# 384 rows of w_out loaded apart, by two queues, with other engines and another order of use

## The chip, the core and the metric

One Trainium2 chip, of which the program uses one core. The metric is the device time of the program in microseconds (us). A core has TensorE (PE in the profile, with its weight loads as PEld), VectorE (DVE), ScalarE (ACT), GpSimd (POOL) and SyncE (SP), and 16 DMA engines that all queues share. SP and ACT issue transfers through hardware queues (q1 and q10 in the profile), GpSimd through a software queue (q0). q8 and q14 carry instruction packets, which the program does not issue.

## The reference

A single token `x` (1 x 576, bfloat16) is normalised and goes through two branches, whose results are added to it.

```python
xn = layernorm(x)                                  # 576
# A: attention with a window of the cache
q  = xn @ wq                                       # 576 -> 32 heads x 128
k, v = k_cache[:, :, -4096:], v_cache[:, :, -4096:]  # 16 kv heads, each for 2 heads
a  = softmax(q k^T * 128**-0.5) v                  # 32 x 128
A  = a.reshape(4096) @ wo                          # -> 576
# B: gated MLP
z  = gelu(xn @ w_in)                               # 576 -> 4608
z1, z2 = z[:2304], layernorm(z[2304:])
B  = (z1 * (w_sp * z2 + b_sp)) @ w_out             # 2304 -> 576
out = x + A + B
```

Nearly all bytes are weights and cache that are read once: wq, the windows of k and v, w_in, wo and w_out, 51 MB together.

## The kernel before, in words

**Loads.** Everything large is loaded by SP, in one order written out by hand at the top of the kernel: wq in two loads, k0, k1, v0, k2, v1, k3, win, v2, v3, wo in two loads, and w_out in four (`load`, line 96). The four k and v blocks hold four kv heads each. Two pools of two buffers each hold these tiles (`small` and `large`); a load waits until the tile that had its buffer before has been read. So `wo` waits for the last z product, which reads `win`, and `wout` for the last transposition of k3. A transfer of 128 partitions is shared out over all 16 DMA engines, eight partitions each.

**w_out.** SP loads rows 384 to 2303 (before: 256 to 2303), with partition p holding FR consecutive rows side by side. In before that is FR = 16 rows a partition, cut after 8, 13 and 15. The first rows of w_out are loaded apart: in before GpSimd loads 160 of them to partitions 64 to 79 (line 393) and ScalarE 96 to partitions 0 to 11 (line 396), both to columns behind the other FR rows. These columns are zeroed first by GpSimd (line 391), since TensorE reads all 128 partitions of them. Two very small transfers of GpSimd (`skip`, line 388) write to columns that nothing reads; they stand ahead of its load and behind it.

**Stages.** For each block b, `turn(b)` transposes k on VectorE (line 214), `scores(b)` makes the scores and the softmax (lines 259 to 285), `weigh(b)` multiplies the weights with v (line 293) and copies the sum to SBUF on ScalarE (line 298), and `heads(b)` adds up the parts of each head (line 304) and scales it on VectorE (line 307). The calls stand in a fixed order, and each engine works through its own instructions in the order of the program:

turn 0, scores 0, turn 1, scores 1, values 0 (weigh and heads), turn 2, scores 2, values 1, turn 3, the zeroing and GpSimd's transfers, scores 3, ScalarE's transfer, `z_all`, weigh 2, `gate`, heads 2, the rows of w_out loaded apart, values 3, o_x and o_p (the attention's output as columns), the 32 rows of wo, the FR rows of w_out, the output.

**z and gate.** `z_all` multiplies the token with w_in in nine rounds r (line 323). Four column groups of TensorE (`tile_position`) take 512 columns each; the columns that belong to the 256 rows apart go to a second PSUM tile, 96 in group 0 and 160 in group 2. VectorE copies the results to SBUF (lines 332 and 334) into 32 x 32 blocks and transposes these (lines 338 and 339), so that z stands by partition as w_out does; row j of a 32 x 32 block comes out as partition j. `gate` computes the gelu, the second norm and the product `hv`, one column for each of the FC = 26 row sets.

**The sum.** `row_of` (line 406) adds one row set to the output: two matmuls of a column with 288 columns of weights each, in two column groups, into two PSUM tiles `fin`. The last row set of w_out closes the sum; VectorE and ScalarE copy the two halves (lines 430 and 431), and SP and ScalarE store them.

Of the kernel before, what the change touches and what calls it, by code (L numbers as in the profile page):

```python
# [8 lines left out]
FP32 = mybir.dt.float32  # L9
# [5 lines left out]
P = 128  # L15
D = 576
# [5 lines left out]
FH = 2304  # L22
# [7 lines left out]
EPS = 1e-5  # L30
SCALE = DH ** -0.5
GELU_C = 0.7978845608028654
FR = 16
FA, RA = 96, 8
FB, RB = 160, 10
FE = FA + FB
FC = FR + RB
FQ = 512
WR = HQ * DH // P
HW = D // 2  # L40
ZPAD = 24
# [6 lines left out]
def kernel(  # L48
# [14 lines left out]
    nc = tc.nc  # L63
# [4 lines left out]
    one = ctx.enter_context(tc.tile_pool(name="one", bufs=1))  # L68
# [19 lines left out]
    def unit(name, width):  # L88
        pool = small if width == SMALL else large
        return pool.tile([P, width], BF16, name=name, tag="u")  # L90
# [4 lines left out]
    def load(t, view, width, cuts):  # L95
        for a, e in zip(cuts, cuts[1:]):
            nc.sync.dma_start(t[:, (a - cuts[0]) * width:(e - cuts[0]) * width], view[:, a * width:e * width])
# [23 lines left out]
    wo_t = unit("wo", LARGE)  # L121
    load(wo_t, wo_v, D, (0, 20, WR))
    wout_t = unit("wout", SMALL)
    load(wout_t, B_w_out[FE:FH, :].rearrange("(p r) n -> p (r n)", r=FR), D, (0, 8, 13, 15, FR))


    ident = const.tile([P, P], BF16, name="ident")
# [1 line left out]
    xw = const.tile([P, NR, 32], BF16, name="xw")  # L129
# [46 lines left out]
    def rstd_of(stats_ps, n, name):  # L176
        mv = const.tile([P, 4], FP32, name=name)
        nc.vector.tensor_scalar_mul(mv[:, 0:2], stats_ps, 1.0 / n)
        nc.vector.tensor_mul(mv[:, 2:3], mv[:, 0:1], mv[:, 0:1])
        nc.vector.tensor_sub(mv[:, 2:3], mv[:, 1:2], mv[:, 2:3])  # L180
        nc.scalar.activation(mv[:, 2:3], mv[:, 2:3], ACT.Ln, bias=eps_t[:, 0:1])
        nc.scalar.activation(mv[:, 3:4], mv[:, 2:3], ACT.Exp, scale=-0.5)
        return mv
# [103 lines left out]
    def weigh(b):  # L287
        pv = ps_v.tile([P, 512], FP32, name=f"pv{b}", tag="pv")
        v4 = vn[b][:, 0:NU * DH].rearrange("p (k n u d) -> p k u n d", k=2, n=4, d=DH)
        for kk in range(2):  # L290
            for u in range(UK):
                g = u % 4
                nc.tensor.matmul(  # L293
                    pv[32 * g:32 * g + 32, :].rearrange("p (n d) -> p n d", n=4), lhsT=p_t[b][:, kk, u, :],
                    rhs=v4[:, kk, u, :, :], start=kk == 0 and u < 4, stop=kk == 1 and u >= UK - 4,
                    tile_position=(0, 32 * g))
        pvs = one.tile([P, 512], FP32, name=f"pvs{b}", tag="pvs")
        nc.scalar.copy(pvs[:], pv[:])  # L298
        return pvs

    def heads(b, pvs):
        op = ps_m.tile([P, 8], FP32, name=f"op{b}", tag="m")
        for u in range(4):
            nc.tensor.matmul(op[:], lhsT=pvs[:, DH * u:DH * (u + 1)], rhs=selu[:, 8 * u:8 * u + 8],  # L304
                             start=u == 0, stop=u == 3)
        with nc.allow_low_precision(reason="the attention's output is bfloat16 in the reference"):
            nc.vector.tensor_tensor(out=o_t[:, 8 * b:8 * b + 8], in0=op[:], in1=rms[b][:], op=ALU.mult)  # L307

    def values(b):
        heads(b, weigh(b))  # L310


    hv = const.tile([P, FC], BF16, name="hv")


    def z_all():
        zs = one.tile([P, FQ + 32 * RB], FP32, name="zs", tag="sm")
        nc.gpsimd.memset(zs[:, FQ:], 0.0)
        zx = zs[:, FQ:].rearrange("p (r i) -> p r i", i=32)
        zp = [ps_a.tile([P, FQ], FP32, name=f"z{i}", tag="a") for i in range(2)]  # L320

        def product(i, g, r, a, n, to):
            nc.tensor.matmul(zp[i][32 * g:32 * g + 32, to:to + n], lhsT=xw[:, r, :],  # L323
                             rhs=win_t[:, FH * r + a:FH * r + a + n],
                             start=r == 0, stop=r == NR - 1, tile_position=(0, 32 * g))

        for r in range(NR):
            for g in range(4):
                product(0, g, r, FE + FQ * g, FQ, 0)
            product(1, 0, r, 0, FA, 0)  # L330
            product(1, 2, r, FA, FB, FA)
        nc.vector.tensor_copy(zs[:, 0:FQ], zp[0][:])
        for q, n, a, rows, k in ((0, 12, 0, RA, 3), (64, 16, FA, RB, 4)):
            nc.vector.tensor_copy(
                zx[q:q + 32, 0:rows, 0:n].rearrange("p r (i x) -> p r i x", x=4),
                zp[1][q:q + 32, a:a + n * rows].rearrange("p (x i r) -> p r i x", x=4, i=k))
        zt = one.tile([P, FC, 32], FP32, name="zt", tag="zt")
        nc.vector.transpose(zt[:, 0:FR, :], zs[:, 0:FQ].rearrange("p (i r) -> p r i", r=FR))
        nc.vector.transpose(zt[:, FR:, :], zx)
        return zt[:, :, 0:2]  # L340

    def gate(z):
        def t3(name):
            return const.tile([P, FC, 2], FP32, name=name)

# [8 lines left out]
        nc.vector.reciprocal(e[:], e[:])  # L354
        G = const.tile([P, 2, FC], FP32, name="G")
        nc.vector.tensor_mul(G[:].rearrange("p h c -> p c h"), e[:], z)
        sz = const.tile([P, 2], FP32, name="sz")
        nc.vector.tensor_reduce(out=sz[:, 0:1], in_=G[:, 1, :], axis=AXX, op=ALU.add)
        jz = const.tile([P, FC], FP32, name="jz")
        nc.vector.tensor_tensor_reduce(out=jz[:], in0=G[:, 1, :], in1=G[:, 1, :], scale=1.0, scalar=0.0,  # L360
# [3 lines left out]
        mz = rstd_of(sp[:], FH, "mz")  # L364
        gz = const.tile([P, FC], FP32, name="gz")
        nc.vector.tensor_scalar(out=gz[:], in0=G[:, 1, :], scalar1=mz[:, 0:1], scalar2=mz[:, 3:4],
# [14 lines left out]

    def blocks(a, e, k):
        return B_w_out[a:e, :].rearrange("(x i r) n -> i x (r n)", x=4, i=k)

    def skip(k, a):
        nc.gpsimd.dma_start(wout_t[0:k, a:a + 32].rearrange("i (m c) -> i m c", m=2),
                            B_w_out[0:2 * k, 0:16].rearrange("(m i) n -> i m n", m=2))

    nc.gpsimd.memset(wout_t[:, D * FR:D * FC], 0.0)  # L391
    skip(8, D * FC)
    nc.gpsimd.dma_start(wout_t[64:80, D * FR:D * FC], blocks(FA, FE, 4))
    skip(4, D * FC + 32)
    scores(3)
    nc.scalar.dma_start(wout_t[0:12, D * FR:D * (FR + RA)], blocks(0, FA, 3))
    z = z_all()
    pvs2 = weigh(2)
    gate(z)
# [4 lines left out]
    def row_of(col, w, start=False, stop=False):  # L404
        for g in range(2):
            nc.tensor.matmul(fin[g][32 * g:32 * g + 1, :], lhsT=col, rhs=w[:, HW * g:HW * (g + 1)],  # L406
                             start=start, stop=stop, tile_position=(0, 32 * g))

    row_of(one_bf[:, 0:1], x_row, start=True)
    for r in range(FR, FC):  # L410
        row_of(hv[:, r:r + 1], wout_t[:, D * r:D * (r + 1)])
    values(3)


    o_x = const.tile([P, 32], BF16, name="o_x")
# [47 lines left out]
```

## Time and profile before

| | |
|---|---|
| median of 3 runs | 127.32 us (127.17 to 127.56) |
| the profiled execution | 127.1 us |
| its span, from the first to the last instruction | 125.3 us |
| mean granted TensorE clock | 0.845 |
| busy: PE, DVE, POOL, ACT | 62%, 52%, 9%, 8% of the span |
| bytes read | 50.96 MB, 407 GB/s over the span |

The profile shows one execution. Its busy slices cut the span into 40 equal parts and give each engine's busy share in tenths. The chain of waits is followed back from the last instruction: at each step to what released it. A line of the timeline is start, duration, engine, source line, operation and tile. The DMA rows are mean shares over 16 engines. The trace also keeps every DMA packet with its start, duration, bytes and queue, and the time of every semaphore increment that a transfer leaves.

### The profile page before, as it was taken

The numbers are of one execution on the slowest core, as the hardware profiler recorded it, in microseconds if no ns is written. First come the engines' busy times: TensorE is split into PE (matmuls) and PEld (weight loads), VectorE is DVE, ScalarE is ACT, GpSimd is POOL, SyncE is SP. The second block draws the span as 40 slices with busy tenths as digits, with TensorE's granted clock in tenths as the row PEclk, the third lists the DMA queues.
The fourth block names the chain that finished last, engine by engine and source line by source line (L and its number), as shares of the span: only waits on it lengthen the run. The fifth ranks groups of instructions, "written<-read, shape, count | busy, mean of one in ns | idle before, by whom it ended". The sixth has DMA issues, their size and how long they took to land.

```text
span 125.3 us, 1324 instructions
## 1 busy us (share of the span) xinstructions
PE 77.9 (62%) x528; PEld 39.3 (31%) x532; DVE 65.0 (52%) x131; ACT 10.2 (8%) x19; POOL 11.0 (9%) x15
## 2 busy tenths in 40 slices
PE   0233550099823999197499637499459434977971
PEld 0231220034311333044234224134148222543640
DVE  6336033499839994340899541999540952001001
ACT  3010000000030000301000031000030110010001
POOL 8400000000000000000000000000992000000000
PEclk9999999999996579855559999779995995586798
DMA  3999899997989989899998999999898999999960
GB/s 107 511 430 439 353 502 418 418 492 345 502 377 447 481 366 481 366 471 429 418 492 356 520 434 424 416 388 471 377 481 359 467 394 433 449 393 415 410 260 0
DMA packets 2624, 51.03 MB, mean 407 GB/s; under 512 B 411, under 2 KB 543, under 8 KB 799
## 3 DMA queue, kind: packets, MB, share of 16 engines
q1 hardware_dynamic: 2450, 50.66, 94.7%
q0 software_dynamic: 144, 0.19, 0.4%
q10 hardware_dynamic: 25, 0.11, 0.2%
q8 instruction: 4, 0.07, 0.2%
q14 instruction: 1, 0.01, 0.0%
HBM read 50.96 MB, written 0.00 MB: 407 GB/s over the span
## 4 chain that ended last, share of the span: by engine, by line
PE 43%; DMA 36%; DVE 10%; ACT 4%; issue 3%; SPq 1%; ACTq 0%
PE s L259 29%; DMA wout<-in_B_w_out_dram 18%; DMA k<-in_A_k_cache_dram 18%; PE pv L293 4%; DVE kt L214 4%; PE z L323 3%; ACT p L279 3%; PE op L304 2%; DVE sm L262 2%; PE tr L270 2%; PE fin L406 1%; PE su L283 1%; DVE pt L281 1%; DVE m L272 1%; ACT pvs L298 1%
## 5 line engine op out<-in xcount | busy, mean ns | idle before, releaser
L259 PE MATMUL s<-kt,zq 128*128 128x512 bf16 x124 | 36.8, 458 | 11.8 <-DVE kt L214 11.1
L214 DVE STREAM_TRANSPOSE kt<-k 128x1024 f32<-128x1024 f32 x32 | 36.4, 1206 | 3.9 <-DMA k<-in_A_k_cache_dram 3.9
L259 PEld LDWEIGHTS <-zq 128*128 128x128 bf16 x128 | 14.5, 113 | 33.0 <-issue 22.4
L391 POOL MEMSET wout<- 128x5760 bf16 x1 | 4.9, 4897 | 83.2 <-DVE kt L214 83.2
L293 PE MATMUL pv<-v,pt 128*32 128x512 bf16 x128 | 11.9, 498 | 0.0
L279 ACT ACTIVATE p<-sm,nm 128x1024 bf16<-128x1024 f32 x4 | 4.6, 1147 | 69.9 <-DVE nm L275 69.9
L307 DVE TENSOR_TENSOR o_t<-op,rm 128x8 bf16<-128x8 f32 x4 | 0.7, 165 | 16.6 <-PE op L304 16.6
L281 DVE STREAM_TRANSPOSE pt<-p 128x1024 bf16<-128x1024 bf16 x4 | 5.0, 1245 | 5.4 <-ACT p L279 5.4
L262 DVE CUSTOM_DVE_ANT_1 sm<-s,cm 128x512 f32<-128x512 f32 x8 | 5.4, 673 | 4.0 <-PE s L259 4.0
L223 PE MATMUL q_ps<-wq,xw 128*32 128x512 bf16 x36 | 4.2, 626 | 4.7 <-DMA wq<-in_A_wq_dram 2.4
L293 PEld LDWEIGHTS <-pt 128*32 128x32 bf16 x128 | 5.7, 119 | 3.8 <-issue 2.4
L304 PE MATMUL op<-selu,pvs 128*128 128x8 f32 x32 | 5.1, 287 | 2.5 <-ACT pvs L298 2.1
L283 PE MATMUL su<-sel,l 128*128 128x8 f32 x8 | 1.8, 292 | 7.7 <-ACT p L279 7.7
L406 PE MATMUL fin<-wout,hv 128*1 128x288 bf16 x52 | 5.1, 344 | 2.3 <-DMA wout<-in_B_w_out_dram 2.3
L304 PEld LDWEIGHTS op<-selu,pvs 128*128 128x128 f32 x32 | 4.8, 228 | 4.4 <-ACT pvs L298 4.0
L406 PE MATMUL fin<-wo,o_p 128*1 128x288 bf16 x64 | 5.7, 353 | 0.3 <-DVE o_p L420 0.3
L430 DVE CAST res<-fin 1x288 bf16<-1x288 f32 x1 | 0.4, 446 | 8.8 <-PE fin L406 8.8
L161 PE MATMUL x_ps<-one_bf,x_row 1*64 1x1 bf16 x9 | 1.2, 248 | 5.6 <-DMA x_row<-in_A_x_dram 5.6
L323 PE MATMUL z<-win,xw 128*32 128x512 bf16 (+2 forms) x54 | 4.4, 448 | 0.0
L270 PE MATMUL tr<-ident_f,m 128*128 128x128 f32 x8 | 1.9, 326 | 3.9 <-DVE m L268 3.9
L406 PEld LDWEIGHTS <-o_p 128*1 128x1 bf16 x64 | 3.3, 101 | 3.1 <-DVE o_p L420 1.0
L406 PEld LDWEIGHTS <-hv 128*1 128x1 bf16 x52 | 2.6, 95 | 4.5 <-issue 3.0
(94 smaller groups left out, 44.4 us busy)
## 6 DMA issues: line engine op xcount, KB each, us to landing
k<-in_A_k_cache_dram SPq DMA_DIRECT2D x4, 4096.0 KB, 21.5
v<-in_A_v_cache_dram SPq DMA_DIRECT2D x4, 4096.0 KB, 26.6
win<-in_B_w_in_dram SPq DMA_DIRECT2D x1, 5184.0 KB
wq<-in_A_wq_dram SPq DMA_DIRECT2D x1, 3584.0 KB, 12.8
wo<-in_A_wo_dram SPq DMA_DIRECT2D x1, 2880.0 KB
wo<-in_A_wo_dram SPq DMA_DIRECT2D x1, 1728.0 KB, 19.4
wout<-in_B_w_out_dram SPq DMA_DIRECT2D x1, 1152.0 KB
wq<-in_A_wq_dram SPq DMA_DIRECT2D x1, 1024.0 KB, 4.8
```

Of the source, the lines that this page charges most:

```text
L214: nc.vector.transpose(t[:].rearrange("p c n e -> p (c n e)").bitcast(FP32), kn[b][:, UK * DH * k:UK * DH * (k + 1)].bitcast(FP32).rearrang ...
L223: nc.tensor.matmul(q_ps[32 * g:32 * g + 32, :], lhsT=xw[:, r, :], rhs=wq_t[:, 2048 * r + 512 * g:2048 * r + 512 * (g + 1)], start=r == 0, ...
L259: nc.tensor.matmul(s_ps[:], lhsT=zq[:, b, ce, ZPAD - 8 * k4:ZPAD - 8 * k4 + P], rhs=kt[b, 4 * kk + k4][:, c, :, e], start=k4 == 0 and ce = ...
L262: nc.vector.tensor_tensor_reduce(out=sm[:, kk, :].rearrange("p (n s) -> p n s", s=HB), in0=s_ps[:].rearrange("p (n s) -> p n s", s=HB), in ...
L270: nc.tensor.matmul(tr[:], lhsT=m1[:].to_broadcast([P, P]), rhs=ident_f[:], start=True, stop=True)
L279: nc.scalar.activation(p[:], sm[:].rearrange("p k n -> p (k n)"), ACT.Exp, bias=nm[:], accum_out=l[:])
L281: nc.vector.transpose(p_t[b][:].rearrange("p k u m -> p (k u m)"), p[:])
L293: nc.tensor.matmul(pv[32 * g:32 * g + 32, :].rearrange("p (n d) -> p n d", n=4), lhsT=p_t[b][:, kk, u, :], rhs=v4[:, kk, u, :, :], start=k ...
L304: nc.tensor.matmul(op[:], lhsT=pvs[:, DH * u:DH * (u + 1)], rhs=selu[:, 8 * u:8 * u + 8], start=u == 0, stop=u == 3)
L323: nc.tensor.matmul(zp[i][32 * g:32 * g + 32, to:to + n], lhsT=xw[:, r, :], rhs=win_t[:, FH * r + a:FH * r + a + n], start=r == 0, stop=r = ...
L391: nc.gpsimd.memset(wout_t[:, D * FR:D * FC], 0.0)
L406: nc.tensor.matmul(fin[g][32 * g:32 * g + 1, :], lhsT=col, rhs=w[:, HW * g:HW * (g + 1)], start=start, stop=stop, tile_position=(0, 32 * g))
```

## The change

- Instead of 256 rows of w_out, 384 are loaded apart, to ten columns sets behind the others as before. SP's loads get one row a partition less (FR = 15, cut after 8, 12 and 14).
- GpSimd's load takes 200 rows to 20 partitions (60 to 79) in place of 160 to 16. The first `skip` is of 7 instead of 8 and now comes ahead of the zeroing.
- ScalarE's one load of 96 rows becomes three: 80 rows to partitions 0 to 19, 72 rows to partitions 0 to 11, and 32 rows to partitions 96 to 127, one row each.
- The zeroing writes the same bytes as 32-bit words: 2,880 elements a partition instead of 5,760.
- In `z_all` the columns of the rows apart are one product of 384 columns in column group 0, ahead of the four products of 480 in each round. Three copies on VectorE and two on ScalarE (a share that crosses a boundary of 32 partitions is cut in two) bring them into the blocks, in place of two on VectorE.
- The ten row sets apart are added behind the fourth values' products: five between `weigh(3)` and `heads(3)`, five after `heads(3)`. Before, all ten stood ahead of `weigh(3)`.

```diff
-FR = 16
-FA, RA = 96, 8
-FB, RB = 160, 10
-FE = FA + FB
-FC = FR + RB
-FQ = 512
+FR = 15
+RX = 10
+XA, XB, XC, XD, FE = 0, 80, 152, 352, 384
+FC = FR + RX
+FQ = 32 * FR
...
-    load(wout_t, B_w_out[FE:FH, :].rearrange("(p r) n -> p (r n)", r=FR), D, (0, 8, 13, 15, FR))
+    load(wout_t, B_w_out[FE:FH, :].rearrange("(p r) n -> p (r n)", r=FR), D, (0, 8, 12, 14, FR))
...
         for r in range(NR):
+            product(1, 0, r, 0, FE)
             for g in range(4):
-                product(0, g, r, FE + FQ * g, FQ, 0)
-            product(1, 0, r, 0, FA, 0)
-            product(1, 2, r, FA, FB, FA)
+                product(0, g, r, FE + FQ * g, FQ)
+
+
+        def share(copy, p, row, rows, first, k, i, n):
+            g, j = divmod(p, 32)
+            copy(zx[32 * g:32 * g + 32, row:row + rows, j:j + 4 * n].rearrange("p r (i x) -> p r i x", x=4),
+                 zp[1][0:32, first:first + 4 * k * rows].rearrange("p (x i r) -> p r i x", x=4, i=k)[:, :, i:i + n, :])
+
+        share(nc.scalar.copy, 64, 0, 10, XC, 5, 1, 4)
+        share(nc.scalar.copy, 60, 0, 10, XC, 5, 0, 1)
         nc.vector.tensor_copy(zs[:, 0:FQ], zp[0][:])
-        for q, n, a, rows, k in ((0, 12, 0, RA, 3), (64, 16, FA, RB, 4)):
-            nc.vector.tensor_copy(
-                zx[q:q + 32, 0:rows, 0:n].rearrange("p r (i x) -> p r i x", x=4),
-                zp[1][q:q + 32, a:a + n * rows].rearrange("p (x i r) -> p r i x", x=4, i=k))
+        share(nc.vector.tensor_copy, 0, 0, 4, XA, 5, 0, 5)
+        share(nc.vector.tensor_copy, 0, 4, 6, XB, 3, 0, 3)
+        nc.vector.tensor_copy(zx[96:128, 0, :], zp[1][0:32, XD:FE])
...
-    def blocks(a, e, k):
-        return B_w_out[a:e, :].rearrange("(x i r) n -> i x (r n)", x=4, i=k)
+    def apart(p, row, rows, first, k):
+        return (wout_t[p:p + 4 * k, D * (FR + row):D * (FR + row + rows)],
+                B_w_out[first:first + 4 * k * rows, :].rearrange("(x i r) n -> i x (r n)", x=4, i=k))
...
-    nc.gpsimd.memset(wout_t[:, D * FR:D * FC], 0.0)
-    skip(8, D * FC)
-    nc.gpsimd.dma_start(wout_t[64:80, D * FR:D * FC], blocks(FA, FE, 4))
+    skip(7, D * FC)
+    nc.gpsimd.memset(wout_t[:, D * FR:D * FC].bitcast(FP32), 0.0)
+    nc.gpsimd.dma_start(*apart(60, 0, 10, XC, 5))
     skip(4, D * FC + 32)
     scores(3)
-    nc.scalar.dma_start(wout_t[0:12, D * FR:D * (FR + RA)], blocks(0, FA, 3))
+    nc.scalar.dma_start(*apart(0, 0, 4, XA, 5))
+    nc.scalar.dma_start(*apart(0, 4, 6, XB, 3))
+    nc.scalar.dma_start(wout_t[96:128, D * FR:D * (FR + 1)], B_w_out[XD:FE, :])
     z = z_all()
...
-    for r in range(FR, FC):
+    pvs3 = weigh(3)
+    for r in range(FR, FR + 5):
         row_of(hv[:, r:r + 1], wout_t[:, D * r:D * (r + 1)])
-    values(3)
+    heads(3, pvs3)
+    for r in range(FR + 5, FC):
+        row_of(hv[:, r:r + 1], wout_t[:, D * r:D * (r + 1)])
```

More of the change, by code (lines that the diff above doesn't have):

```diff
@@ L316, in z_all @@
     def z_all():
-        zs = one.tile([P, FQ + 32 * RB], FP32, name="zs", tag="sm")
+        zs = one.tile([P, FQ + 32 * RX], FP32, name="zs", tag="sm")
         nc.gpsimd.memset(zs[:, FQ:], 0.0)
@@ L320, in z_all, with product @@
         zp = [ps_a.tile([P, FQ], FP32, name=f"z{i}", tag="a") for i in range(2)]
-        def product(i, g, r, a, n, to):
-            nc.tensor.matmul(zp[i][32 * g:32 * g + 32, to:to + n], lhsT=xw[:, r, :],
+        def product(i, g, r, a, n):
+            nc.tensor.matmul(zp[i][32 * g:32 * g + 32, 0:n], lhsT=xw[:, r, :],
                              rhs=win_t[:, FH * r + a:FH * r + a + n],
```

## The prediction, as it was recorded

> **What bounds the kernel now.** I read the busy slices and the DMA queues first, then the chain that ended last, then the single view of the tile `wout`, and last the trace's own packet records.
>
> ```profile
> DMA  3999899997989989899998999999898999999960
> ...
> q1 hardware_dynamic: 2450, 50.66, 94.7%
> ```
>
> The DMA engines are busy from the second slice to the last but one; SP's queue alone takes 94.7% of 16 engines' span. The chain of waits ends there too:
>
> ```profile
> 98.28 23.00 DMA wout<-in_B_w_out_dram
> 121.28 0.04 issue
> 121.32 1.40 PE fin L406 x16
> 122.72 0.44 DVE res L430
> ```
>
> ```profile
> L406 PE MATMUL fin<-wout,hv x52: 282/286/444, 105.9 to 122.4; 128*1 128x288 bf16 x52
> ```
>
> The 1.40 us are not one run of 16 matmuls. At full clock a pair starts every 0.12 us, and the last pair starts at 122.39: in the trace's matmul rows ten follow 121.28, four start at 122.09 and two at 122.39. Row 15's load landed at 122.35, rows 13 and 14 at 122.05. So **the end is the last landing plus 0.04 us, one matmul of 0.28 us and the fixed rest**. TensorE is nearly ready then, not quite the bound: its rows 0 to 7 ran from 119.54 to 120.69 and it then stood 0.63 us.
>
> **Which DMA engine is last.** The trace keeps each packet's start, duration, bytes and queue, not its engine. On one engine a packet begins 3 to 4 ns before the last one's recorded end, so the packets sort into 16 chains. A transfer also leaves one semaphore increment per engine; those of row 15's load came at 120.48, .56, .71, .72, then 121.31, then 121.70 to 122.35 (eleven). By the chains:
> - three carry ACT's load (four packets of 9,216 B, 0.35 us each: +1.41 us) and four POOL's (four of 11,520 B, 0.434 us: +1.74 us);
> - nine carry neither. Four of them are on time. One is 1.0 us late since an instruction packet of 8 KB at 38.7 us, four are 1.4 to 1.6 us late, each since one instruction packet of 16 KB (39.1, 79.2, 99.8, 118.7 us).
>
> The 64-byte packets of the two skips place them: the skip of 8 falls on the three ACT chains and five others, POOL's load on four more, the skip of 4 on the last four. So POOL's transfers go on from where the last one ended. Of the late chains two are among the last four; the 8 KB one and those of 99.8 and 118.7 are among the five unloaded of the first eight, beside two on time.
>
> **The change, part by part.** In the listing of the built kernel its transfers have leading sizes 20 over 5 (POOL), 20 over 5, 12 over 3 and 32 (ACT); before they were 16 over 4 on four engines and 12 over 3 on three, so I take 5, 5, 3 and 16 engines.
> - *SP, all engines*: one row less, in the second load (4 rows for 5). 5,760 B took 222 ns and 2,304 B 94, so 4,608 B is some 179: 8 x (222 - 179) = **-0.34 us**. The third ACT load puts two packets of 1,152 B on each engine: 2 x 51 ns = **+0.10**.
> - *POOL's engines*: again four packets of 434 ns each. The four old ones, last at 122.35, gain 0.24: **122.11**.
> - *ACT's first three*: 4 x 179 + 4 x 264 (6,912 B, same slope) = 1.77 for 1.41, less 0.24: +0.12. They were at 121.70 to about 121.98: at most **122.10**.
> - *The two late ones of the last four*: 122.3 - 0.24 = **122.06**.
> - *ACT's two new engines*: 0.72 - 0.24 = +0.48. On time 121.2, the 8 KB one 121.8, the 118.7 one 122.3 to 122.4, the 99.8 one 122.6.
> - *POOL's fifth engine*, the last of the first eight: 1.74 - 0.24 = +1.50. On time 122.0 to 122.2; if late, see the first rival.
>
> Everything else has to stay under that cover:
> - *z products*: the busiest column group does 480 + 384 columns a round for 512 + 160. The old 9 x 672 took 0.87 us at clock 1.0 and 3.42 at 0.5 (the windows view), 2,344 columns a us at full clock; 1,728 more are 0.74 us at full clock, 1.5 at half, 0 if all groups shared the work (the total is 2,304 columns both times). I take 0.74, as the clock was 1.0 from 96.79. It delays SP's load of wo, which waits for the last read of `win`, from 96.95 to 97.7; the engines have v3 until 103.3, so 5 us hide it, and past that each us is a us. hv comes at about 105.3 for 104.5, and TensorE now wants it after the fourth values, at 109.4.
> - *Copies*: DVE three small ones for two (0.24 and 0.32 us before): 0 to +0.4 us. ACT two new ones, 0.24 (like DVE's 32x96) to 0.58 (its 128x512): 0.5 to 1.2 us, at 97.6; what follows on ACT, the pvs copy and the Exp, feeds heads(2), which TensorE ran at 102.8. Hidden by over 2 us.
> - *Memset*: 4.90 us for 5,760 elements; for 2,880 of four bytes 2.45 (by elements) to 4.90 (by bytes). I take 2.45. Only ACT's and POOL's loads hang on it, which then start earlier; the engines' sum is the same.
> - *Three ACT issues* for one of 0.81: 1.3 to 2.4 us from 92.2, before the copies at 97.6. Free.
> - *SP's last two loads* take over semaphores of ACT's first two and now wait for their landings, about 103 and 108. The engines reach them at some 119. Free by 10 us; if not, the engines run dry one for one.
> - *Rows moved behind the fourth values' products*: these start when v3 lands (105.80, not 107.58) and end at about 109.4. Then comes the **new wait**: the first moved row needs all three ACT loads. ACT's queue got one packet per packet of SP's (97.09, 98.67, 100.24, 101.81, the receipt 103.37). Now 4 + 1 + 4 + 1 + 2 + 1 = 13 turns, ten at 1.2 us and less: 109.4 to 110.3, seen 0.45 later. TensorE stands until 109.8 to 110.8, with heads(3) queued behind it and DVE's o_t, o_x and o_p behind that. Ten matmuls (0.6 us), op (1.06), the other ten (0.6, beside o_t and o_x, 0.38), op_ps and o_p (0.4): wo starts at 112.7 to 113.9, before at 113.97. No loss, and the gain meets loads that set the pace anyway.
>
> **Sum**: last landing 122.11 for 122.35, -0.24 us, on the profiled run's 127.1 us (span 125.3 and 1.8 around it): 126.9. The median of three was 127.32, so **127.1** is the forecast, and 126.8 to 127.4 its own range. It could only be -0.7 if all 16 engines ended together: the mean of the 16 increments is 121.7.
>
> **Rivals.**
> 1. *POOL's fifth engine is a late one* (slower). Price: it holds +1.50 on top of its own lateness. The 8 KB one landed at 121.31, so 122.8; the other two at 121.9 and 122.1, so 123.4 to 123.6: +0.5 to +1.2 us, 127.8 to 128.5. It decides once that engine is over 0.3 us late. For it: of the five possible chains three are late. Against: chains differ in phase; v2 ended on ACT's three at 93.45 to 93.62, on POOL's four at 93.58 to 93.76, on the last four (lateness taken off) at 93.57 to 93.85, so roughly by number, and the last in phase of the five, 93.76, is on time. The Trainium skill (DMA: Bandwidth & Descriptors, Latency and other measured facts) says that engines 7 and 15 are usually slower than the rest, and its section on why a DMA increments its semaphore by 16 that a software transfer takes consecutive engines from a cursor, which would make engine 7 the fifth; by that rule this rival holds. The trace shows late engines in both halves but no numbers. Chance 0.22.
> 2. *The 99.8 engine gets ACT's new share*: 122.57, +0.2: 127.5. Chance 0.07.
> 3. *TensorE is late*: ACT's loads come two turns later than I count, the stand lasts past 111.5, wo starts after 114.6, its slack of 0.6 is gone: 0.4 to 1.0 us slower, 127.7 to 128.3. For it: 13 turns with a packet between. Against: 59 ns a matmul at full clock lets it catch up. Chance 0.06.
> 4. *The change doesn't spread as its sizes say*, for example POOL's load on all 16 engines (0.54 us each): the latest chains at 122.3 + 0.30, 127.5; or only the order changes: 127.3. Chance 0.07.
>
> **How the numbers follow.** Forecast 0.58. A difference of 0.3% (0.38 us) is about what a measurement of this kernel can tell from none. The forecast's -0.24 lies inside, but the three runs shown spread over 0.39 us and the engines' lateness may move by some tenths: I give 0.30 of the 0.58 to faster, 0.28 to same. Same: 0.28 + 0.07 + 0.05 of rival 4 = 0.40. Slower: 0.22 + 0.06 + 0.02 = 0.30. The range runs from 126.7 (a gain of 0.6) to 127.9 (the cheap end of rivals 1 and 3); outside lie the dear half of rival 1 and little else.
>
> **What would show it.** Right: 16 increments of the last load closer together, the last near 122.1; 20 POOL packets of 11,520 B on five chains; the last pair of matmuls 0.04 us after the last landing; TensorE standing 0.4 to 1.3 us at the first moved row. Wrong: one increment alone far behind (rival 1), a last pair long after its landing (rival 3), engines idle before SP's last loads (the semaphores), the clock at 0.5 after 117.3 (a pair in 0.24 us).

## The result, and the profile after

The changed kernel took **127.74 us** (median of 6, 127.67 to 127.86) against 127.30 (median of 6, 127.17 to 127.56): a ratio of **1.0035, 95% interval 1.0022 to 1.0048**. It is 0.44 us slower, where -0.2 was forecast. The profiled execution took 127.84 us with a span of 126.0 (before 127.1 and 125.3); these two single executions lie 0.74 us apart, the medians 0.44.

The busy slices and the queues of the changed kernel, then the end of its chain of waits (start, duration, what):

```profile
DMA  3999999998999989999899999999999999999960
...
q1 hardware_dynamic: 2450, 50.51, 94.1%
q0 software_dynamic: 144, 0.23, 0.5%
q10 hardware_dynamic: 98, 0.21, 0.4%
```

```profile
90.25 11.70 DMA wout<-in_B_w_out_dram
101.95 0.02 issue
101.97 20.34 DMA wout<-in_B_w_out_dram
122.31 0.04 issue
122.35 0.62 PE fin L415 x6
122.98 0.44 DVE res L442
```

The kernel is bound as before: the DMA engines are busy to the end, the last loads of w_out land, six matmuls follow, and `res` is copied 0.26 us later than before (122.98 for 122.72). The chain's step through ScalarE's first load (90.25, landed 101.95) to SP's issue at 101.97 is real but decides nothing: the engines reach that load some 18 us later.

The sum over w_out, by the single view of the tile, starts later and ends later:

```profile
L415 PE MATMUL fin<-wout,hv x50: 282/285/286, 109.8 to 122.7; 128*1 128x288 bf16 x50
```

The semaphore increments of SP's last load come at 120.76 to 121.20 (four engines) and 122.04 to **122.60** (twelve); before, the last came at 122.35. That is +0.25 where the sum had -0.24. From the copy to the end of the span there is a second loss: 126.0 - 122.98 is 3.0 us, before 125.3 - 122.72 was 2.6. So two things are to be explained: **about half a microsecond in the landing, and 0.4 us behind it**, where the prediction had a "fixed rest".

### The profile page after: what moved, and what is told of

The parts are those of the page before. It is cut to its first block, busy times and chain, and to the rows that moved or that the text cites. A ratio compares the mean times of both kernels' runs of the same rounds, so it can differ in the third digit from the quotient of the medians.

```text
span 126.0 us, 1311 instructions
## 1 busy us (share of the span) xinstructions
PE 77.0 (61%) x521; PEld 36.8 (29%) x521; DVE 64.9 (52%) x132; ACT 10.7 (8%) x21; POOL 8.7 (7%) x15
## 4 chain that ended last, share of the span: by engine, by line
DMA 43%; PE 31%; DVE 15%; ACT 4%; POOL 3%; issue 1%; SPq 1%; ACTq 0%
DMA wout<-in_B_w_out_dram 25%; PE s L258 23%; DMA k<-in_A_k_cache_dram 18%; DVE kt L213 10%; PE pv L292 4%; ACT p L278 3%; PE op L303 2%; POOL wout L399 2%; DVE sm L261 2%; PE tr L269 1%; DVE pt L280 1%; ACT pvs L297 1%; DVE m L271 1%; SPq L96 1%; PE su L282 1%
## 5 line engine op out<-in xcount | busy, mean ns | idle before, releaser
L258 PE MATMUL s<-kt,zq 128*128 128x512 bf16 x128 | 37.4, 460 | 10.9 <-DVE kt L213 10.9
L292 PE MATMUL pv<-v,pt 128*32 128x512 bf16 x128 | 10.1, 466 | 1.6 <-DMA v<-in_A_v_cache_dram 1.6
L395 POOL DMA_DIRECT2D wout<-in_B_w_out_dram x2 | 1.3, 640 | 82.5 <-DVE kt L213 82.5
L303 PE MATMUL op<-selu,pvs 128*128 128x8 f32 x32 | 5.8, 310 | 1.8 <-ACT pvs L297 1.4
L303 PEld LDWEIGHTS op<-selu,pvs 128*128 128x128 f32 x32 | 5.5, 259 | 3.5 <-ACT pvs L297 3.1
L415 PE MATMUL fin<-wo,o_p 128*1 128x288 bf16 x64 | 4.2, 286 | 2.4 <-DMA wo<-in_A_wo_dram 2.4
L292 PEld LDWEIGHTS <-pt 128*32 128x32 bf16 x128 | 3.9, 110 | 5.6 <-issue 2.1
L322 PE MATMUL z<-win,xw 128*32 128x480 bf16 (+1 forms) x45 | 5.1, 475 | 0.0
L415 PE MATMUL fin<-wout,hv 128*1 128x288 bf16 x50 | 3.9, 285 | 1.6 <-DMA wout<-in_B_w_out_dram 1.4
L282 PEld LDWEIGHTS su<-sel,l 128*128 128x128 f32 x8 | 1.4, 218 | 8.4 <-ACT p L278 8.4
```

Source lines behind the costliest of these rows:

```text
L258: nc.tensor.matmul(s_ps[:], lhsT=zq[:, b, ce, ZPAD - 8 * k4:ZPAD - 8 * k4 + P], rhs=kt[b, 4 * kk + k4][:, c, :, e], start=k4 == 0 and ce = ...
L282: nc.tensor.matmul(su[:], lhsT=l[:].to_broadcast([P, P]), rhs=sel8[:], start=True, stop=True)
L292: nc.tensor.matmul(pv[32 * g:32 * g + 32, :].rearrange("p (n d) -> p n d", n=4), lhsT=p_t[b][:, kk, u, :], rhs=v4[:, kk, u, :, :], start=k ...
L322: nc.tensor.matmul(zp[i][32 * g:32 * g + 32, 0:n], lhsT=xw[:, r, :], rhs=win_t[:, FH * r + a:FH * r + a + n], start=r == 0, stop=r == NR - ...
```

## Experiments

Each time stands beside that of the kernel before on the same chip (127.08 to 127.29 us, by the chip). "Tail" is the time from the landing of SyncE's store to the end of the span. "v3 stage" is the time of one DMA engine from its last packet of v2 to its last of v3, taken on the plain engines: those that carry nothing of GpSimd and of ScalarE's first two loads and no instruction packet (the median of the three to seven of these that the packets' records let one follow). Theory A is that the order of SyncE's waits at the close makes the tail longer; theory B, that ScalarE's third load costs the engines more than its bytes. Rivals were the new order of the rows, and other new waits.

### The tail: which semaphores the stores get

A semaphore is a counter that a transfer raises when it has landed, and that an engine waits for. The view of SyncE's waits from 120 us on, before and after:

```profile
SPq L458 <- DMA out_dram<-res: 0.4, 1, 0.4
```

```profile
SPq L470 <- DMA out_dram<-res: 0.9, 1, 0.9
```

At its end SyncE waits for all DMA semaphores in turn, about 60 ns each, as the trace's records of its instructions show:

```
before (SP's store holds 110, ScalarE's 109)   after (SP's store holds 102, ScalarE's 100)
124.25  wait 109, 101                          124.71  wait 102
124.43  wait 110, 108                          124.77  wait 103, 100
124.50  first drain                            124.83  wait 104, 113
                                               124.89  wait 105, 112
                                               124.95  wait 107, 111
                                               125.01  wait 109, 101
                                               125.08  wait 110, 108
                                               125.14  first drain
```

The hardware queues' transfers take their semaphores in turn from a set of eight (100, 102, 103, 104, 105, 107, 109 and 110 in both kernels). With two more transfers the stores came to the first places of the closing order. Before, SyncE did the five waits ahead of these while the stores were under way (123.56 to 123.81); after, it stops at the first one, and six still follow the store's landing: 6 x 0.06 = 0.37 us.

**b_plus2**: the kernel before with two spare loads of one element, early, on ScalarE.

```diff
+    spare = const.tile([1, 2], BF16, name="spare")
+    for i in range(2):
+        nc.scalar.dma_start(spare[:, i:i + 1], B_w_sp.flatten_outer_dims()[0:1, 0:1])
```

> The kernel before plus two spare loads of one element each on ScalarE at the start: nothing else changes, but the output stores get the semaphores that they have in the changed kernel. Theory of the closing waits: 0.37 us slower than before, 127.65 to 127.70, ratio 1.003; 1.24 us from the store's landing to the end in place of 0.87. Rival (the loss lies in the queues): 127.3, ratio 1.000.

Measured: 127.68 against 127.29, ratio 1.003 (1.0021 to 1.0039). Its tail is 1.26 us, and SyncE's wait for the stores 0.9 us:

```profile
SPq L461 <- DMA out_dram<-res: 0.9, 1, 0.9
```

**b_plus1**: the same with one spare load, so that the stores' semaphores move by one place only.

> The kernel before with one spare load of one element by ScalarE at the start, so that the stores' semaphores move by one place in the order of SyncE's closing waits: SyncE's store then holds one of the first two places. Closing waits: a tail of about 1.2 us from the landing of SyncE's store to the end of the span, for 0.91, and 127.5 to 127.7. If the 0.39 us of the version with two spare loads came from the loads themselves, half of it: 127.45 with the tail at 0.91.

Measured: 127.52 against 127.08, ratio 1.0034 (1.0022 to 1.0046), tail 1.19. One spare load costs no less than two, so the cost does not go by the number of loads but with the place in the order. The tail does not hold all of it: it is 0.28 us longer with one spare load and 0.35 with two, and in both profiled executions the last landing is later as well (122.54 and 122.49 for 122.35). What made the landing later was not taken apart; with before's own loads it came at 122.42 in b_rows_behind.

**a_plus6**: the changed kernel with six spare loads, so that the set comes round and the stores hold the last places again.

```diff
+    spare = const.tile([1, 6], BF16, name="spare")
+    for i in range(6):
+        nc.scalar.dma_start(spare[:, i:i + 1], B_w_sp.flatten_outer_dims()[0:1, 0:1])
```

> The changed kernel plus six spare loads of one element each on ScalarE at the start, so that both output stores are given the two semaphores that SyncE waits for last at the end of the program, as in the kernel before. Theory (the store's semaphore stands first in the closing waits, six waits of about 60 ns follow its landing): 0.37 us less than the changed kernel's 127.74, so 127.35 to 127.40, ratio to before 1.000 to 1.002; the span from the landing of SyncE's store to the end falls from 1.24 to 0.87 us. Rival (the later last landing, 122.60 for 122.35, and what hangs on it make the whole loss): 127.7 as before this edit.

Measured: 127.65 against 127.29, ratio 1.0028 (1.0018 to 1.0037). The tail is back at 0.91, but the gain over the changed kernel is only 0.09 where 0.34 to 0.39 was expected: one engine was last by itself at 122.80, the others at 122.45 and earlier. That it is the one with the spare packets is the likely reading and was not shown: behind the last of them, at some 23 us, one engine trails the sixth of the 16 by 0.64 us, where in before and after the latest trails it by 0.28 and 0.51. If so, the spare loads take back by an engine most of what they give at the close.

**a_minus2**: so the opposite way, the changed kernel with two transfers fewer.

```diff
-    for a in range(0, D, D // 2):
-        nc.scalar.dma_start(x_row[:, a:a + D // 2], A_x.flatten_outer_dims()[:, a:a + D // 2])
+    nc.scalar.dma_start(x_row[:], A_x.flatten_outer_dims())
...
-load(wq_t, wq_v, 2048, (0, 2, NR))
+load(wq_t, wq_v, 2048, (0, NR))
```

> The changed kernel with x loaded in one load instead of two and wq in one instead of two, so that two transfers less give both output stores the semaphores that SyncE waits for last, without spare packets on the first DMA engine (in the run with six spare loads one engine's last landing came 0.35 us after the fifteen others). Theory of the closing waits: 0.37 us less than the changed kernel, 127.35 to 127.45, the last landing as in the changed kernel (122.6) and 0.9 us from the store's landing to the end. Rival (that run's 127.65 is what the semaphores are worth): 127.65.

Measured: 127.47 against 127.23, ratio 1.002 (1.0011 to 1.0029), tail 0.90, last landing 122.70. The gain over the changed kernel is 0.2 to 0.27 us, less than the 0.37 of the waits, and the landing is 0.10 later than there. It remains slower than before: theory A holds and isn't all.

### The landing: ScalarE's third load

**a_no_third**: the changed kernel without the load of 32 rows to partitions 96 to 127 (these rows are left out of the sum); one spare load keeps the semaphores where the change has them.

```diff
-    nc.scalar.dma_start(wout_t[96:128, D * FR:D * (FR + 1)], B_w_out[XD:FE, :])
```

> The changed kernel without ScalarE's third load (its 32 rows of w_out are left out of the sum: those partitions stay zero) and with one spare load in its place, so that all semaphores stay as in the changed kernel. If the third load costs each engine 0.32 us, as the packet records of the changed kernel make it (v2's end to the landing of rows 0 to 7 is 23.89 us on an engine with nothing else, 23.57 before): last landing 0.3 us earlier, 127.4 to 127.45. If it costs its own two packets, 0.10 us: 127.64. The closing waits stay at 1.24 us after the store's landing in both.

Measured: 127.39 against 127.29, ratio 1.0002 (0.9993 to 1.001). The last landing is at 122.10, where the prediction's sum without its 0.10 for this load has 122.01, and the tail remains at 1.27.

**a_third_own** and **a_third_step**: the same 36,864 bytes by the same queue, but spread over all partitions, to columns that nothing reads (the 32 rows are left out of the sum). The first writes 288 B to each of 128 partitions, the second one row to every fourth partition.

```diff
-    nc.scalar.dma_start(wout_t[96:128, D * FR:D * (FR + 1)], B_w_out[XD:FE, :])
+    nc.scalar.dma_start(wout_t[:, D * FC + 64:D * FC + 64 + 144], B_w_out[XD:FE, :].rearrange("r (q c) -> (r q) c", q=4))
```

```diff
-    nc.scalar.dma_start(wout_t[96:128, D * FR:D * (FR + 1)], B_w_out[XD:FE, :])
+    nc.scalar.dma_start(wout_t[0:128:4, D * FC + 64:D * FC + 64 + D], B_w_out[XD:FE, :])
```

> The changed kernel with its third ScalarE load replaced by one of the same 36.9 KB to columns that nothing reads, spread over all 128 partitions (288 bytes each), so that each engine writes the partitions that it writes in SyncE's loads, in eight packets instead of two; its 32 rows are left out of the sum. If the price of the third load is that its two packets an engine go to partitions 96 to 127, which in SyncE's loads other engines write: cheap, 127.4 to 127.5. If the price hangs on the number of packets and turns: dearer than the changed kernel, 128.0 or more. If it is the bytes: 127.4 to 127.5 too, and then the next run tells it.

> The changed kernel with its third ScalarE load sent to columns that nothing reads, on every fourth partition (0, 4, 8 and so on) instead of 96 to 127: the same 32 packets of 1,152 bytes, two on each engine, but evenly over the partitions; its 32 rows are left out of the sum. If the price comes from many engines writing to partitions 96 to 127: 127.4 to 127.5. If it comes from the packets, wherever they go: 127.7 as the changed kernel.

Measured: 127.44 (ratio 1.0015, 1.0003 to 1.0027) and 127.45 (1.0014, 1.0005 to 1.0023), both against 127.23 and both with the long tail. The stages of the engines set them apart from the change:

| | v3 stage, us | wo to rows 0 to 7 of w_out, us | last landing |
|---|---|---|---|
| before | 9.76 | 13.81 | 122.35 |
| after: rows to partitions 96 to 127 | 10.03 | 13.87 | 122.60 |
| a_minus2: the same load | 9.99 | 13.90 | 122.70 |
| a_plus6: the same load | 9.95 | 13.86 | 122.80 |
| a_no_third | 9.77 | 13.78 | 122.10 |
| a_third_own | 9.92 | 13.80 | 122.31 |
| a_third_step | 9.88 | 13.78 | 122.34 |

Two packets of 1,152 B more cost an engine about 0.1 us when they are spread (a_third_step, 0.12 - 0.03), as the prediction had it; eight of 288 B (a_third_own) cost 0.16 - 0.01. The same bytes to 32 partitions in a row cost 0.27 in the first stage and 0.06 in the second in the changed kernel (0.24 to 0.33 together in the three runs with this load), and SP's packets beside them take longer (eight of 32,768 B together 9.91 us for 9.74). The last column says less than the stages: it moves by some 0.1 us between executions with the same large loads (before 122.35, b_rows_behind 122.42; after 122.60, a_minus2 122.70).

**b_far**: the suspected cause by itself and larger. The kernel before, with ScalarE's one load (108 KB on three engines) on partitions 20 to 31 instead of 0 to 11, and VectorE's copy to match.

```diff
-    nc.scalar.dma_start(wout_t[0:12, D * FR:D * (FR + RA)], blocks(0, FA, 3))
+    nc.scalar.dma_start(wout_t[20:32, D * FR:D * (FR + RA)], blocks(0, FA, 3))
```

> The kernel before with ScalarE's one load moved from partitions 0 to 11 to partitions 20 to 31 (and the copy of z with it): the same packets on the same three DMA engines, but into partitions that in SyncE's loads three other engines write. Theory (a load apart is cheap only where its engines write the partitions they write in SyncE's loads): SyncE's packets get longer than 9.75 us for eight of v3 on some engines, the last landing comes 0.2 us or more later, 127.5 or more. Rival (the third load of the changed kernel was dear because all 16 engines wrote to the same 32 partitions; where three engines write is no matter): 127.3.

Measured: **128.58** against 127.24, ratio 1.0103 (1.0088 to 1.0117). Not three engines are late but all: the plain ones need 10.89 us for the v3 stage instead of 9.76. The last matmuls run to 124.0:

```profile
L406 PE MATMUL fin<-wout,hv x52: 283/286/448, 105.7 to 124.0; 128*1 128x288 bf16 x52
```

### The order of the rows, and versions that might be better

**b_rows_behind**: the kernel before with only the rows apart moved behind the fourth values' products, as the change does.

```diff
-    for r in range(FR, FC):
+    pvs3 = weigh(3)
+    for r in range(FR, FR + 5):
         row_of(hv[:, r:r + 1], wout_t[:, D * r:D * (r + 1)])
-    values(3)
+    heads(3, pvs3)
+    for r in range(FR + 5, FC):
+        row_of(hv[:, r:r + 1], wout_t[:, D * r:D * (r + 1)])
```

> The kernel before with only the order of use changed: its ten row sets loaded apart are added behind the fourth values' products, five ahead of the heads and five behind. If the last landing sets the end, no change: 127.3, ratio 0.999 to 1.001, with TensorE waiting longer before the last rows. If TensorE's order was part of the loss: slower by 0.1 us or more.

Measured: 127.27 against 127.29, ratio 1.0002 (0.9991 to 1.0014). The order costs nothing that can be told from the noise (0.18 us at most by the interval).

**v_11rows**: no third load. GpSimd loads 220 rows (11 a partition), ScalarE 80 and 84, and x comes in one load, so that the stores hold the last semaphores.

```diff
-RX = 10
-XA, XB, XC, XD, FE = 0, 80, 152, 352, 384
+RX = 11
+XA, XB, XC, FE = 0, 80, 164, 384
...
-    nc.gpsimd.dma_start(*apart(60, 0, 10, XC, 5))
+    nc.gpsimd.dma_start(*apart(60, 0, 11, XC, 5))
...
-    nc.scalar.dma_start(*apart(0, 4, 6, XB, 3))
-    nc.scalar.dma_start(wout_t[96:128, D * FR:D * (FR + 1)], B_w_out[XD:FE, :])
+    nc.scalar.dma_start(*apart(0, 4, 7, XB, 3))
```

> A version after both findings: no third load; its 32 rows go into the two other kinds (GpSimd 220 rows in 11 a partition, ScalarE 80 and 84 rows), and x in one load, so that the count of transfers gives the stores the last two semaphores. GpSimd's five engines carry four packets of 12,672 bytes, 1.91 us, less 0.34: 0.17 us earlier than before's last landing of 122.35. Theory: 127.1 to 127.2, ratio to before 0.998 to 0.999. If the five engines include a late one or SyncE's loads suffer as in the changed kernel: 127.4 or more.

Measured: 127.13 against 127.23, ratio 0.9993 (0.9984 to 1.0001): not to be told from no change. Last landing 122.37, tail 0.91: GpSimd's engines, which carry 11 rows a partition for 10, came last and set the end.

**v_step**: the changed kernel with the 32 rows as an eleventh row set on every fourth partition, x in one load, the scalar b_sp loaded by GpSimd (which moves the semaphores), and the first skip reduced to 6, on the belief that this load takes one engine of the software queue.

```diff
-    nc.scalar.dma_start(ws2[:, 1:2], B_b_sp.flatten_outer_dims()[0:1, 0:1])
+    nc.gpsimd.dma_start(ws2[:, 1:2], B_b_sp.flatten_outer_dims()[0:1, 0:1])
...
-        nc.vector.tensor_copy(zx[96:128, 0, :], zp[1][0:32, XD:FE])
+        for g in range(4):
+            nc.vector.tensor_copy(zx[32 * g:32 * g + 32, RX - 1, 0:32:4], zp[1][0:32, XD + 8 * g:XD + 8 * g + 8])
...
-    skip(7, D * FC)
+    skip(6, D * FC)
...
-    nc.scalar.dma_start(wout_t[96:128, D * FR:D * (FR + 1)], B_w_out[XD:FE, :])
+    nc.scalar.dma_start(wout_t[0:128:4, D * (FC - 1):D * FC], B_w_out[XD:FE, :])
```

> The changed kernel with its third ScalarE load put on every fourth partition as an eleventh row set, used as the last of those apart, x in one load, and one bias scalar loaded by GpSimd instead of ScalarE (the first skip is one smaller for it), so that the stores have the last two semaphores. The balance of the prediction should come out: last landing 0.2 us before 122.35, 127.0 to 127.1, ratio to before 0.998 to 0.999. Rival (something else in the changed kernel costs as well): 127.3 or more.

Measured: **129.63** (129.02 to 130.55) against 127.24, ratio 1.0195 (1.016 to 1.023). A clear miss. Its engines show b_far's sign, 11.00 us for the v3 stage. The suspicion was that the load of b_sp takes no engine, so that the skip of 6 put GpSimd's 225 KB one engine too low.

**v_step2** changes one number back:

```diff
-    skip(6, D * FC)
+    skip(7, D * FC)
```

> The changed kernel with the 32 rows of the third ScalarE load as an eleventh row set on every fourth partition, x in one load, b_sp loaded by GpSimd, and the first skip of 7 as in the change (of 6 in the failed version, which counted the load of b_sp as one place of the cursor). If that load takes no place, GpSimd's load is back on the engines of its own partitions: plain engines 9.8 to 9.9 us for the v3 stage, last landing 122.2 to 122.4, tail 0.91 us, time 127.0 to 127.2, a ratio of 0.998 to 1.000. If the place was counted rightly and the failure came from the eleventh row set, the engines' stage stays at 10.9 us and the time at 128.5 or above.

Measured: **126.88** (126.80 to 127.54) against 127.08, ratio **0.9988 (0.9978 to 0.9998)**. Last landing 122.14, tail 0.91, v3 stage 9.86. The chain's end:

```profile
121.82 0.69 PE fin L415 x6
122.51 0.44 DVE res L442
```

This pair is also the cleanest test of what lies behind theory B, that a load apart can cost more than its bytes: both kernels write the same rows to the same partitions with the same queues, and differ in which engines carry GpSimd's load. The table by stretches of time (length, busy time and instructions of PE, PEld, DVE, ACT and POOL, then granted clock, DMA share and GB/s), first of v_step, then of v_step2, b_far and before:

```profile
94.00:104.00 10.00, 7.29 (x77) 3.02 (x69) 4.25 (x16) 1.29 (x4) 0.00 (x0) 0.76 0.98 364
```

```profile
94.00:104.00 10.00, 5.72 (x63) 2.70 (x58) 5.40 (x22) 1.32 (x5) 0.00 (x0) 0.84 1.00 423
```

```profile
94.00:104.00 10.00, 5.05 (x49) 3.07 (x45) 6.03 (x22) 1.23 (x4) 0.00 (x0) 0.84 1.01 377
```

```profile
94.00:104.00 10.00, 6.22 (x74) 4.99 (x67) 5.39 (x20) 1.33 (x4) 0.79 (x2) 0.84 0.98 418
```

The DMA engines are equally busy in all four (0.98 to 1.01), but move 364 and 377 GB/s in v_step and b_far, and 423 and 418 in v_step2 and before. In v_step more came on top: a GpSimd engine that was also late by an instruction packet landed last, at 124.94 (the others by 123.81), and TensorE ran its last 30 matmuls at half the clock:

```profile
122.47 3.70 PE fin L415 x30
```

How much of the 2.75 us between v_step and v_step2 (2.59 when each is set against before on its own chip) each of these has was not taken apart.

## Why the prediction was wrong

Two steps failed, both of them terms that were taken as small or fixed. The 127.74 lies inside the stated range of 126.7 to 127.9, but that is luck: the upper end came from rivals that did not happen, and the direction was wrong.

**"The last landing plus 0.04 us, one matmul of 0.28 us and the fixed rest."** The rest isn't fixed. It holds SyncE's closing waits, and their length behind the stores hangs on which semaphores the stores drew. The prediction counted the hardware transfers' semaphores where SP's last loads took over ScalarE's, and did not follow the same count to the stores. Size: +0.37 us by the waits (the tail goes from 0.91 to 1.27); b_plus2 and b_plus1 got 0.35 and 0.28 of tail, and 0.39 and 0.44 us in all. This alone turns the forecast's sign (-0.24 + 0.37 = +0.13).

**"The third ACT load puts two packets of 1,152 B on each engine: 2 x 51 ns = +0.10."** The packets were priced by their bytes and the partitions they write were not looked at. By the stages it is 0.27 + 0.06 = 0.33 us in the changed kernel, so the term was about 0.23 too small (0.14 in a_plus6, the cheapest of the three runs with this load); taking that load's whole price out (a_no_third) gave 127.39 for 127.74, against the same kernel before within 0.01 us.

**What held: the balance of the engines.** The row that SP saves gave what was forecast: from the last packet of rows 0 to 7 to the last packet of all, a plain engine needs 2.53 to 2.54 us for 2.88 to 2.91 before, some -0.36 where the sum had -0.34. v_step2 has both losses taken away, and its landing at 122.14 meets the 122.11 of the sum, closer than single executions agree, so in part by luck. Its median is 0.20 below before (0.03 to 0.28 by the interval), where -0.24 was forecast. The accounts for the changed kernel: -0.24 (balance) + 0.37 (closing waits) + 0.23 (what the third load costs beyond 0.10) = +0.36, measured +0.44 with an interval of some 0.28 to 0.61. In the profiled runs the landing is 122.60 - 122.11 = 0.49 later than forecast, twice the 0.23; the other part goes with how the engines stood in these two single executions when v2 ended: at 93.98 on the last of GpSimd's engines after, at 93.76 before, and on the latest of all at 95.79 for 95.41. This is a reading of two runs, not a test.

**The parts that were to cost nothing:**
- The zeroing as 32-bit words takes half, as taken (2.45 forecast). ScalarE's three issues take 2.04 us together (1.3 to 2.4 forecast):

```profile
L399 POOL MEMSET wout<- x1: 2517/2517/2517, 87.7 to 87.7; 128x2880 f32 x1
L403 ACTq DMA_DIRECT2D wout<-in_B_w_out_dram x1: 873/873/873, 90.2 to 90.2; - x1
L404 ACTq DMA_DIRECT2D wout<-in_B_w_out_dram x1: 747/747/747, 91.2 to 91.2; - x1
L405 ACTq DMA_DIRECT2D wout<-in_B_w_out_dram x1: 422/422/422, 91.9 to 91.9; - x1
```

- The z products took 5.14 us for 4.31, +0.83 (0.74 forecast). They began 0.97 us earlier (91.53 for 92.50), so SP's load of wo went out at 96.72 and not at 97.7. VectorE's three small copies took 0.54 and ScalarE's two 0.47:

```profile
96.56 0.47 ACT L334 COPY zs<-z 32x160 f32<-32x160 f32 x2 [5.40 <-PE z L322]
96.73 0.66 DVE L339 COPY zs<-z 128x480 f32<-128x480 f32 x1 [4.21 <-PE z L322]
97.31 0.36 DVE L334 COPY zs<-z 32x80 f32<-32x80 f32 x2
97.68 0.18 DVE L342 COPY zs<-z 32x32 f32<-32x32 f32 x1
```

- SP waits for the landings of ScalarE's first two loads, 8.0 us in all, and harmlessly: its last issues come at 101.97 and 106.87, and the engines get there behind 119. The view of SyncE's waits between 96 and 112 us:

```profile
SPq L96 <- DMA wout<-in_B_w_out_dram: 8.0, 2, 4.6
```

- The new wait of TensorE isn't one: the third load had landed at 109.56, when the fourth values' products (from 106.34) were just ending. TensorE then waits for wo and for w_out, that is for the stream. Its timeline (start, duration, line, tile, and the idle time before with its releaser):

```profile
109.81 0.78 PE L415 MATMUL fin<-wout,hv 128*1 128x288 bf16 x10
110.52 1.06 PE L303 MATMUL op<-selu,pvs 128*128 128x8 f32 x8
111.51 0.78 PE L415 MATMUL fin<-wout,hv 128*1 128x288 bf16 x10
112.22 0.19 PE L430 MATMUL op_ps<-o_x,perm 128*128 128x32 bf16 x1
113.25 1.02 PE L415 MATMUL fin<-wo,o_p 128*1 128x288 bf16 x14 [0.84 <-DMA wo<-in_A_wo_dram]
```

The 0.4 to 1.3 us of standing that were forecast did not come, since v3's products began 0.5 us later than reckoned (106.34 for 105.80) and the load's landing was seen at 109.56, ahead of the 109.8 to 110.8 reckoned.

**The rivals.** *POOL's fifth engine late* (0.22) is false: five chains carry GpSimd's 11,520 B packets, all five started on time (v2 ended at 93.67 to 93.98) and needed about 11.7 us for the v3 stage. The rule in the Trainium skill (DMA: Bandwidth & Descriptors, Latency and other measured facts) that engines 7 and 15 are usually slower thus found no support here: no engine of GpSimd's load was slower than the others of it, and the records don't say whether one of them was engine 7. *The 99.8 engine gets ACT's new share* (0.07) did not set the end: here this instruction packet came at 106.3, and ScalarE's two new engines had their last packets by 121.7, the last engine at 122.19. *TensorE late* is false by the timeline above, wo starting at 113.25. *The change doesn't spread as its sizes say* is false: the packets are where the leading sizes said. The slower case came by two mechanisms that no rival named.

## What to carry to other kernels

When a stream of transfers is the bound, price a side load by which partitions it writes and which engines carry it, as well as by its bytes, and read the price from the stages of engines that carry none of it. Here it was cheap where it was spread evenly, or lay, by the reading below, on engines that write the same partitions in the main stream. Follow every count that a change moves, here that of the transfers, to the last instruction: one more transfer cost 0.44 us here (b_plus1), 0.28 of it at the close. And try a failed version's own wrong number before the idea is given up: v_step and v_step2 differ by one digit and 2.75 us.

## What was not expected of the hardware

**A transfer can slow engines that carry none of it.** In b_far 108 KB on three engines cost all 16 some 1.1 us (a packet of 32,768 B took 1.36 us on average for 1.22), and in v_step 225 KB on five cost plain engines the same; with the same bytes one engine further (v_step2) their stage was 9.86, as in a_third_step (9.88). The Trainium skill (DMA: Bandwidth & Descriptors, The descriptor swizzle) says that in a transfer of 128 partitions engines 0 to 7 write partitions 0 to 63, each four of the first 32 and four of the second, and engines 8 to 15 the upper 64 likewise. By that, and with the engines counted as in the prediction, before's loads and v_step2's 60 to 79 lie on the engines' own partitions, b_far's and v_step's do not, and the change's third load crowds the partitions of engines 8 to 15; the times of these runs agree. The records carry no engine numbers, so this assignment is a reading and not shown. Why engines with nothing to do with these partitions slow down as well stays open; so does whether foreign partitions alone suffice, since the third load on every fourth partition, by that rule foreign too but even, cost no more than its bytes.

**A load of one element by GpSimd moved no engine of its queue**, by v_step and v_step2: counting it as one gave 11.00 us for the v3 stage, not counting it 9.86. In v_step2's packets the skip of seven lies on ScalarE's five engines and two more, GpSimd's load on five that carry neither skip, and the skip of four on the last four.
